# An mLSTM cell and a feed-forward block on one core: the first product by Strassen's algorithm in the second chunk too

## The chip, the cores and the metric

The kernel runs on one core of a Trainium2 chip. The metric is the device time of one execution in microseconds; lower is better. The engines are PE (TensorE, matrix products), DVE (VectorE), ACT (ScalarE), POOL (GpSimd) and SP (SyncE, which here only issues transfers). "PEld" in a profile is PE loading the stationary operand of a product.

## The reference

Two blocks follow each other. The first is an mLSTM cell over 4 batches, 8 heads, 768 time steps and head size 40; the second is a product, a sigmoid-approximated GELU and another product over the 3072 resulting rows of 320 numbers.

```python
for t in range(S):                                   # per batch and head
    m_new = maximum(f_gate[t] + m, i_gate[t])
    f_stab, i_stab = exp(f_gate[t] + m - m_new), exp(i_gate[t] - m_new)
    m = m_new
    C = f_stab * C + i_stab * outer(v[t], k[t])      # 40 x 40 state
    n = f_stab * n + i_stab * k[t]
    y[t] = sigmoid(o_gate[t]) * (C @ q[t]) / maximum(abs(n @ q[t]), 1)
x = y as (4*768, 8*40)
h = x @ w_in                                         # 320 x 2048
g = h / (1 + exp(-1.702 * h))
out = g @ w_out                                      # 2048 x 320
```

## The kernel before

**Chunks.** The 768 time steps are cut into NW = 6 chunks (`w`) of 128 steps; a chunk has 4 batches (`b`) of 128 rows, so 512 rows (tokens) of the feed-forward block. Within a chunk the recurrence is written as products: scores of queries and keys, weighted by a matrix of exponentials `wt` that masks the future, times the values, plus the state of the earlier chunks times the queries.

**The order of the work.** It is written out by hand: every engine executes its instructions in the order in which the program names them, and so does SP with its transfers. The main loop at the end of the kernel does, for each chunk `w`, the first product of the feed-forward block (`j` runs over 8 pairs of 128 hidden units), then the second product in blocks (`i`), and between these blocks the attention of chunk `w + 1`, in the steps that `attention(w + 1)` lists and at the block numbers in `stops`. In the first chunk the weights are still being loaded and converted: `fetch(n)` brings raw pieces into staging slots (`big`, six slots of 128 x 1024 numbers, and others), and `convert(n)` turns them into float32 weights with two operations on ACT and four on DVE. `beside` and `weights_in` say which piece is fetched and converted when.

**The first product.** Its contraction is over the 320 columns of a row: two full groups of 128 (`c`) and a rest of 64 (`w_in_x`). In the chunks 0 and 1 `up` computes it plainly: for each pair of hidden units two half columns (`i`) by two groups (`c`), each with all 512 tokens as moving operand. From the chunk 2 on `up_fast` takes Strassen's algorithm (in Winograd's form) for the two full groups: the operands are cut into 2 x 2 blocks (group or hidden half by group, group by token half), and seven products with 256 tokens take the place of eight. It needs sums of weights, `as1`, `as2`, `as4` and `a10` in place (`first_sums`, `first_difference`, made once, while the chunk 1 is worked on), and sums of the chunk's own transposed rows `xT`, `bt1`, `bt2`, `bt4` and `b01` in place (four DVE operations at its start). DVE and ACT add the products up.

**The second product.** In chunk 0 `down(w, b, n)` computes it plainly, in 16 blocks. From chunk 1 on `down_fast` takes Strassen's algorithm, in 7 blocks for each half `c` of the tokens: 14 blocks. It needs sums of weights, `t1`, `t2`, `t4` and `w01` in place (`weight_sums`), and sums of hidden units (`hidden_sums`, DVE). Each block's product goes to one of two banks of `ps_m`; DVE adds it to `o_sb` (line 629, or a copy in line 627), and SP stores the finished rows of one batch (line 633): `store(1)` at block 5 and `store(0)` at block 6 of each half. `o_sb` has two buffers, so the second half (from block 7 on) writes into buffers from which the first half is stored.

**Queries and keys.** `load_blocks(w)` brings the keys and queries of chunk `w` into `k_bl` and `q_bl` with 32 transfers, and `transposes(w, b)` turns one batch of each into `kT` and `qT` on DVE; `k_bl` and `q_bl` have one buffer each, so a chunk's load waits for the transposes of the chunk before it. `gates(w)` computes the running maxima and sends them to DRAM as `m_row`; `spread(w)` brings them back into `wt`, ACT takes the exponentials (line 335), and POOL masks them (line 337). `new_states(w)` (PE) and `carry(w)` (DVE, and a memset on POOL) bring the recurrent state forward: from chunk 2 on as a step of the attention, in chunk 1 in the middle of `up`. `seam(w, b)` transposes the attention's rows into `xT`.

Of the kernel before, what the change touches and what calls it, by code (L numbers as in the profile page):

```python
# [8 lines left out]
FP = mybir.dt.float32  # L9
U32 = mybir.dt.uint32  # L10
BF = mybir.dt.bfloat16
AF = mybir.ActivationFunctionType
OP = mybir.AluOpType
# [21 lines left out]
def kernel(  # L35
# [120 lines left out]
    def fetch(n):  # L156
        if 6 <= n < 10:
            bits[n] = gp.tile([128, 512, 2], U32, tag="g", name="bits")
        else:
            slot = n if n < 6 else (n - 10) % 6  # L160
            bits[n] = big[:, slot, :].bitcast(U32).rearrange("p (a two) -> p a two", two=2)
        for r, c, src in pieces[n][1]:
            dst = bits[n][r, c].rearrange("p a two -> p (a two)")
            if len(src.shape) == 3:
                dst = dst.rearrange("p (j m) -> p j m", j=src.shape[1])
            nc.sync.dma_start(out=dst, in_=src)
# [272 lines left out]
    def hidden_of(w, j):  # L439

        if j % 2 == 0:
            for i in range(2):
                gs[w, i * 4 + j // 2] = gp.tile([128, 2, W], FP, tag="g", name="g")
        return [gs[w, i * 4 + j // 2][:, j % 2, :] for i in range(2)]

    w_half = [[w_in_sb[:, c, :].rearrange("p (n h m) -> h p n m", h=2, m=256)[i] for c in range(2)] for i in range(2)]

    def up(w, j, n, states=False):


        x = xT[w].rearrange("p c b t -> p c (b t)")
        begin, end = range(j, j + n // 2), range(j + n // 2, j + n)
        ph = {}

        def take(j, pool, tag):
            ph[j] = [pool.tile([128, W], FP, tag=tag, name="p_h") for _ in range(2)]

        def full(j, first):
            for c in range(2):
                for i in range(2):  # L460
                    T.matmul(ph[j][i], w_half[i][c][:, j // 2, j % 2 * 128:(j % 2 + 1) * 128], x[:, c, :],  # L461
                             start=(first and c == 0), stop=(not first and c == 1))

        def rest(j, first):
            for i in range(2):
                r = slice(i * 64, i * 64 + 64)
                T.matmul(ph[j][i], w_in_x[r, j, :], x[r, 2, :], start=first, stop=not first)

        def gelu(j):
            for i, g in enumerate(hidden_of(w, j)):  # L470
                A.activation(out=g, in_=ph[j][i], func=AF.Gelu_apprx_sigmoid)  # L471

        for k in begin:
            take(k, *((ps_m, "m") if k == j else (ps_x, "x")))
            full(k, True)
        if states:
            new_states(w)
            carry(w)
        for k in begin:
            rest(k, False)  # L480
            gelu(k)
        for k in end:
            if k not in ph:
                take(k, *((ps_x, "x") if n == 2 else (ps_a, "a")))
            rest(k, True)
        for k in end:
            full(k, False)
            gelu(k)

    a00, a01, a10, a11 = w_half[0] + w_half[1]
    as1, as2, as4 = (big[:, i, :].rearrange("p (n m) -> p n m", m=256) for i in (3, 4, 5))

    def first_sums():
        V.tensor_tensor(out=as1, in0=a10, in1=a11, op=OP.add)
        V.tensor_tensor(out=as2, in0=as1, in1=a00, op=OP.subtract)
        V.tensor_tensor(out=as4, in0=a01, in1=as2, op=OP.subtract)

    def first_difference():  # L500
        V.tensor_tensor(out=a10, in0=a00, in1=a10, op=OP.subtract)

    def up_fast(w, j, between=None):
# [83 lines left out]
    w00, w01 = w_out_sb[:, 0:NH, 0:DH], w_out_sb[:, 0:NH, DH:DM]  # L587
    w10, w11 = w_out_sb[:, NH:NF, 0:DH], w_out_sb[:, NH:NF, DH:DM]

    def weight_sums():  # L590
        V.tensor_tensor(out=t1, in0=w01, in1=w00, op=OP.subtract)
        V.tensor_tensor(out=t2, in0=w11, in1=t1, op=OP.subtract)
        V.tensor_tensor(out=w01, in0=w11, in1=w01, op=OP.subtract)
        V.tensor_tensor(out=t4, in0=w10, in1=t2, op=OP.subtract)

    def hidden_sums(w, c, js, *what):

# [48 lines left out]
    def attention(w):  # L646
        if w > 1:

            return [[(columns, w)], [(weights, w, 0), (weights, w, 1)],
                    [(scores, w, 0), (hidden_sums, w - 1, 1, range(4), 3), (scores, w, 1), (weights, w, 2),  # L650
                     (weights, w, 3)],
                    [(values, w, 0), (values, w, 1), (scores, w, 2), (scores, w, 3)] +
                    [(scale, w, b) for b in (0, 1) if w + 1 < NW],
                    [(seam, w, 0), (seam, w, 1), (last_values, w)], [(carry, w)] if w + 1 < NW else [],
                    [(seam, w, 2)], [(seam, w, 3)]]
        steps = [[(columns, w)]]
        for s in range(B + 3):
            step = []
            for lag, f in ((3, seam), (2, values), (1, scores), (0, weights)):
                if 0 <= s - lag < B:  # L660
                    step.append((f, w, s - lag))
            if 0 <= s - 2 < B:
                step.append((scale, w, s - 2))
            steps.append(step)
        return steps

    def last_values(w):
# [95 lines left out]

    def next_keys():
        gates(w + 1)
        transposes(w + 1, 0)
        transposes(w + 1, 1)

    for w in range(NW):
        more = w + 1 < NW  # L770
        for j in range(NF // 2):
            if j % 2 == 0:
                if w:
                    if j % 4 == 0:
                        if w > 1:
                            up_fast(w, j, next_keys if more and j == 0 else None)
                        else:
                            up(w, j, 4, states=(j == 0))
                elif j == 0:
                    weights_in(0)  # L780
                    for pair_ in range(2):
                        for i, g in enumerate(hidden_of(0, pair_)):
                            A.activation(out=g, in_=first[pair_][i], func=AF.Gelu_apprx_sigmoid)
                else:
                    weights_in(j // 2)
                    up(w, j, 2, states=(j == 2))
            if j == 0 and more:
                load(w + 1, "o")
            if w == 0 and j == 0:
                load_blocks(1, 0)  # L790
                spread(1)
            if w == 1 and j == 1:
                weight_sums()
                first_sums()
            if more:
                if w == 1 and j == 0:
                    gates(w + 1)
                if j == 4:
                    if w == 0:
                        load_blocks(1, 1)  # L800
                    load(w + 1, "v")
                    if w:
                        spread(w + 1)
                if j == (4 if w else 6):
                    load(w + 1, "k")
                if w == 1 and 4 <= j < 6:
                    transposes(w + 1, 2 * j - 8)
                    transposes(w + 1, 2 * j - 7)
            if w > 1 and more and j == 3:
                transposes(w + 1, 2)  # L810
                transposes(w + 1, 3)
            if w and j in (3, 7):
                hidden_sums(w, 0, (j // 4 * 2, j // 4 * 2 + 1), 1, 2)
                if j == 3:
                    hidden_sums(w, 0, (0, 1), 3, 4)
        side = attention(w + 1) if more else []
        if w == 0:

            blocks = [(lambda b=b, n=n: down(w, b, n)) for ns in ((0, 1), (2,), (3,)) for b in range(B) for n in ns]
            stops = (0, 1, 5, 7, 9, 11, 13, 15)  # L820
        else:
            blocks = down_fast(w, 0) + down_fast(w, 1)
            stops = (0, 1, 2, 4, 8, 10, 11, 12)
        for i, block in enumerate(blocks):
            if w == 0:
                weights_in(4 + i)
                for b in {2: (0, 1), 7: (2,), 9: (3,)}.get(i, ()):
                    transposes(1, b)
            elif w + 2 < NW and i == 0:
                load_gates(w + 2)  # L830
                load_blocks(w + 2)
            block()
            if i in stops and side:
                run(side.pop(0))
            if w:
                for at, c, *what in ((0, 0, (2, 3), 3), (1, 0, (2, 3), 4), (1, 1, range(4), 1),
                                     (5, 1, range(2), 2), (6, 1, range(2, 4), 2), (7, 1, range(4), 4)):
                    if i == at:
                        hidden_sums(w, c, *what)
                if i == 2 and not more:  # L840
                    hidden_sums(w, 1, range(4), 3)
            if w == 1 and i == 9:
                first_difference()
        if w == 0:
            load_gates(2)
            load_blocks(2)


# [28 lines left out]
```

## Time and profile before

| | us |
|---|---|
| median of 13 runs | 492.01 |
| lowest and highest of them | 490.89, 495.15 |
| the profiled execution | 491.46 |
| its span in the profile | 489.8 |
| busy: PE, PEld | 482.5, 387.2 |
| busy: DVE, ACT, POOL | 328.8, 211.0, 60.7 |

Stretches of the profiled execution, as PE's timeline shows them, in microseconds from the start of the span:

| stretch | from | to | length |
|---|---|---|---|
| second product of chunk 0, with the attention of chunk 1 | 65.93 | 114.57 | 48.64 |
| first product of chunk 1 (plain) | 115.14 | 151.73 | 36.59 |
| second product of chunk 1, with the attention of chunk 2 | 151.73 | 195.92 | 44.19 |
| first product of chunk 2 (Strassen) | 195.92 | 228.02 | 32.10 |
| second product of chunk 2, with the attention of chunk 3 | 228.02 | 272.20 | 44.18 |

How to read profile lines: a timeline row gives start, length, engine, line of the kernel, operation, output <- inputs, shape and the number of instructions merged into the row; in brackets is how long the engine idled before it, and what ended that idle time. "SPq" is SP's queue of transfers; its length is the time of issue, not of the transfer. The slices of the page show the busy share of each engine in 40 equal parts of the span, in tenths.

### The profile page before, as it was taken

Reading aid. Unit: us, or ns where it says so; the run is one execution under the profiler, and the core shown is the slowest. Engines: PE = TensorE matmul, PEld = TensorE weight load, DVE = VectorE, ACT = ScalarE, POOL = GpSimd, SP = SyncE. Lnnn points to the kernel's source line nnn. Section 1 sums busy time; section 2 is a strip of 40 time slices with the busy share of each in tenths; the row PEclk is TensorE's granted clock in tenths of the full one; section 3 lists DMA queues with packets and bytes.
Section 4 is the critical chain, followed back from the end, with each engine's and each line's share of the span. In section 5 each row is a group of like instructions: output and inputs, shape, how many; then the busy total and the mean of one; then the engine's idle time right before and its main releaser. Section 6 shows DMA issues by size and latency. Waiting matters only on the chain. (4 is left out here: it accounts for less than half of the span.)

```text
span 489.8 us, 10267 instructions
## 1 busy us (share of the span) xinstructions
PE 482.5 (99%) x4028; PEld 387.2 (79%) x4028; DVE 328.8 (67%) x819; ACT 211.0 (43%) x535; POOL 60.7 (12%) x103
## 2 busy tenths in 40 slices
PE   8999999999999999999999999999999999999997
PEld 4874456774447999777999877999977999877897
DVE  8789765872983766677786596677666786254831
ACT  6766766301315600466800374900364930255300
POOL 4030001231000340000322000232000120000000
PEclk9999999999999999999999999999999999999999
DMA  9999799403699610896200696300294000000000
GB/s 132 182 277 352 90 271 168 55 28 63 74 240 132 75 32 15 127 239 67 27 28 3 103 257 80 33 29 2 63 264 37 2 1 28 28 0 3 0 28 27
DMA packets 175952, 44.85 MB, mean 92 GB/s; under 512 B 164352, under 2 KB 169504, under 8 KB 175904
## 3 DMA queue, kind: packets, MB, share of 16 engines
q1 hardware_dynamic: 175904, 44.21, 48.1%
q8 instruction: 31, 0.51, 0.4%
q14 instruction: 17, 0.14, 0.1%
HBM read 40.17 MB, written 4.01 MB: 90 GB/s over the span
## 5 line engine op out<-in xcount | busy, mean ns | idle before, releaser
L624 PE MATMUL p_out<-w_out_sb,g 128*128 128x160 f32 x480 | 69.8, 301 | 0.0
L624 PEld LDWEIGHTS p_out<-w_out_sb,g 128*128 128x128 f32 x480 | 66.4, 190 | 1.3 <-issue 0.5
L400 ACT COPY xT<-p_x 128x384 f32<-128x384 f32 x24 | 11.0, 481 | 128.4 <-PE p_x L399 128.4
L533 DVE TENSOR_TENSOR g<-p_u,g 128x256 f32<-128x256 f32 x64 | 27.2, 425 | 40.8 <-PE p_u L525 32.8
L337 POOL TENSOR_SCALAR_AFFINE_SELECT wt<-wt 128x1024 f32<-128x1024 f32 x20 | 22.5, 1123 | 226.8 <-ACT wt L335 195.8
L461 PE MATMUL p_h<-xT,w_in_sb 128*128 128x512 f32 x112 | 49.9, 599 | 0.6 <-ACT xT L400 0.6
L530 ACT COPY g<-p_u 128x256 f32<-128x256 f32 x96 | 34.5, 378 | 34.5 <-PE p_u L525 31.2
L629 DVE TENSOR_TENSOR o_sb<-o_sb,p_out 128x160 f32<-128x160 f32 x70 | 21.4, 317 | 41.2 <-PE p_out L624 40.9
L335 ACT ACTIVATE wt<-wt,cols 128x128 f32<-128x128 f32 x160 | 48.0, 395 | 0.0
L537 ACT ACTIVATE g<-g 128x256 f32<-128x256 f32 x96 | 33.9, 427 | 31.3 <-DVE g L533 31.3
L461 PEld LDWEIGHTS p_h<-xT,w_in_sb 128*128 128x128 f32 x112 | 20.7, 190 | 28.8 <-issue 26.8
L573 PE MATMUL p_out<-w_out_sb,g 128*128 128x320 f32 x128 | 36.2, 437 | 0.0
L350 DVE TENSOR_TENSOR wt<-p_s,wt 128x512 f32<-128x512 f32 x48 | 30.5, 683 | 8.4 <-POOL wt L337 6.3
L624 PE MATMUL p_out<-t,big 128*128 128x160 f32 x240 | 35.5, 301 | 0.0
L624 PEld LDWEIGHTS p_out<-t,big 128*128 128x128 f32 x240 | 33.3, 190 | 0.2
L471 ACT ACTIVATE g<-p_h 128x512 f32<-128x512 f32 x28 | 15.8, 598 | 38.1 <-PE p_h L461 20.0
L573 PEld LDWEIGHTS p_out<-w_out_sb,g 128*128 128x128 f32 x128 | 23.8, 190 | 10.1 <-issue 0.5
L525 PE MATMUL p_u<-xT,w_in_sb 128*128 128x256 f32 x128 | 31.2, 382 | 0.0
L525 PE MATMUL p_u<-xs,big 128*128 128x256 f32 x128 | 30.3, 379 | 0.0
L553 PE MATMUL p_u<-xT,w_in_x 64*128 64x512 f32 x64 | 29.6, 602 | 0.0
L553 PE MATMUL p_v<-xT,w_in_x 64*128 64x512 f32 x64 | 29.6, 602 | 0.0
L525 PEld LDWEIGHTS p_u<-xT,w_in_sb 128*128 128x128 f32 x128 | 23.7, 190 | 4.5 <-DVE o_sb L629 1.5
(166 smaller groups left out, 865.6 us busy)
## 6 DMA issues: line engine op xcount, KB each, us to landing
wt<-m_row SPq DMA_DIRECT2D x20, 512.0 KB, 6.7
out_dram<-o_sb SPq DMA_DIRECT2D x24, 160.0 KB, 1.8
eo<-in_o_gate_dram SPq DMA_DIRECT2D x5, 640.0 KB, 5.6
v_st<-in_v_dram SPq DMA_DIRECT2D x5, 640.0 KB, 8.8
k_st<-in_k_dram SPq DMA_DIRECT2D x5, 640.0 KB, 11.3
big<-in_moe_w_in_dram SPq DMA_DIRECT2D x5, 512.0 KB, 6.0
big<-in_moe_w_out_dram SPq DMA_DIRECT2D x8, 320.0 KB, 5.4
k_bl<-in_k_dram SPq DMA_DIRECT2D x40, 64.0 KB, 2.6
```

The lines of the kernel that those rows point to most:

```text
L335: A.activation(out=x[:, h, :], in_=x[:, h, :], func=AF.Exp, scale=-1.0, bias=cols[w][:, b * H + h:b * H + h + 1])
L337: G.affine_select(out=x, in_=x, compare_op=OP.is_ge, fill=0.0, base=0, pattern=[[0, H], [1, L]], channel_multiplier=-1)
L350: V.tensor_tensor(out=wt[w, b][:, :, i, :], in0=pw[i], in1=wt[w, b][:, :, i, :], op=OP.mult)
L461: T.matmul(ph[j][i], w_half[i][c][:, j // 2, j % 2 * 128:(j % 2 + 1) * 128], x[:, c, :], start=(first and c == 0), stop=(not first and c = ...
L525: T.matmul(p[k][:, ts[t]], a[:, k // 2, k % 2 * 128:(k % 2 + 1) * 128], b, start=first, stop=True, skip_group_check=True)
L530: A.copy(out=g[k][i][:, ts[t]], in_=chain[k][:, ts[0]])
L533: V.tensor_tensor(out=g[k][i][:, ts[t]], in0=p[k][:, ts[pt]], in1=g[k][i][:, ts[t]], op=OP.add)
L537: A.activation(out=dst, in_=dst if src is None else src, func=AF.Gelu_apprx_sigmoid)
L553: T.matmul(p[k], w_in_x[r, k, :], x[r, 2, :], start=False, stop=True, skip_group_check=True)
L573: T.matmul(po, gs[w, f // 2][:, f % 2, b * L:(b + 1) * L], w_out_sb[:, f, :], start=(f == 0), stop=(f == NF - 1))
L624: T.matmul(po, a(f), b[:, f, :], start=(f == 0), stop=(f == NH - 1))
L629: V.tensor_tensor(out=dst, in0=x, in1=po, op=OP.add)
```

## The change

The second chunk's first product goes by `up_fast` as well, so its weights' sums are made earlier:

- `first_sums`, with `first_difference` taken into it, runs in chunk 0's second product, ahead of block 2. It writes to other staging slots than before, and piece 19 of the weights, which used one of them, is staged in `xs`.
- `weight_sums` is cut into four calls: three at blocks 12, 14 and 15 of chunk 0's second product, one at `j == 3` of chunk 1's first product.
- `new_states(1)` and `carry(1)` become part of the last step of chunk 1's attention, which runs after the last block of chunk 0.
- Chunk 2's gates are computed at the start of `up_fast` in chunk 1. Its transposes are split: batches 0 and 1 at `j == 3` of chunk 1's first product, batches 2 and 3 ahead of blocks 2 and 3 of its second product.
- `load_gates(2)` goes from behind chunk 0's blocks to ahead of the first of them; `load_gates(3)` and `load_blocks(3)` go from block 0 of chunk 1 to block 4.
- `up` is left for chunk 0 alone and is shortened accordingly.

```diff
@@ -157,8 +157,8 @@
         if 6 <= n < 10:
             bits[n] = gp.tile([128, 512, 2], U32, tag="g", name="bits")
         else:
-            slot = n if n < 6 else (n - 10) % 6
-            bits[n] = big[:, slot, :].bitcast(U32).rearrange("p (a two) -> p a two", two=2)
+            room = xs if n == 19 else big[:, n if n < 6 else (n - 10) % 6, :]
+            bits[n] = room.bitcast(U32).rearrange("p (a two) -> p a two", two=2)
         for r, c, src in pieces[n][1]:
             dst = bits[n][r, c].rearrange("p a two -> p (a two)")
             if len(src.shape) == 3:
@@ -445,15 +445,12 @@
 
     w_half = [[w_in_sb[:, c, :].rearrange("p (n h m) -> h p n m", h=2, m=256)[i] for c in range(2)] for i in range(2)]
 
-    def up(w, j, n, states=False):
-
-
-        x = xT[w].rearrange("p c b t -> p c (b t)")
-        begin, end = range(j, j + n // 2), range(j + n // 2, j + n)
-        ph = {}
-
-        def take(j, pool, tag):
-            ph[j] = [pool.tile([128, W], FP, tag=tag, name="p_h") for _ in range(2)]
+    def up(j, states):
+
+
+        x = xT[0].rearrange("p c b t -> p c (b t)")
+        ph = {k: [pool.tile([128, W], FP, tag=tag, name="p_h") for _ in range(2)]
+              for k, pool, tag in ((j, ps_m, "m"), (j + 1, ps_x, "x"))}
 
         def full(j, first):
             for c in range(2):
@@ -467,37 +464,28 @@
                 T.matmul(ph[j][i], w_in_x[r, j, :], x[r, 2, :], start=first, stop=not first)
 
         def gelu(j):
-            for i, g in enumerate(hidden_of(w, j)):
+            for i, g in enumerate(hidden_of(0, j)):
                 A.activation(out=g, in_=ph[j][i], func=AF.Gelu_apprx_sigmoid)
 
-        for k in begin:
-            take(k, *((ps_m, "m") if k == j else (ps_x, "x")))
-            full(k, True)
+        full(j, True)
         if states:
-            new_states(w)
-            carry(w)
-        for k in begin:
-            rest(k, False)
-            gelu(k)
-        for k in end:
-            if k not in ph:
-                take(k, *((ps_x, "x") if n == 2 else (ps_a, "a")))
-            rest(k, True)
-        for k in end:
-            full(k, False)
-            gelu(k)
+            new_states(0)
+            carry(0)
+        rest(j, False)
+        gelu(j)
+        rest(j + 1, True)
+        full(j + 1, False)
+        gelu(j + 1)
 
 
 
     a00, a01, a10, a11 = w_half[0] + w_half[1]
-    as1, as2, as4 = (big[:, i, :].rearrange("p (n m) -> p n m", m=256) for i in (3, 4, 5))
+    as1, as2, as4 = (big[:, i, :].rearrange("p (n m) -> p n m", m=256) for i in (4, 5, 3))
 
     def first_sums():
         V.tensor_tensor(out=as1, in0=a10, in1=a11, op=OP.add)
         V.tensor_tensor(out=as2, in0=as1, in1=a00, op=OP.subtract)
         V.tensor_tensor(out=as4, in0=a01, in1=as2, op=OP.subtract)
-
-    def first_difference():
         V.tensor_tensor(out=a10, in0=a00, in1=a10, op=OP.subtract)
 
     def up_fast(w, j, between=None):
@@ -587,11 +575,9 @@
     w00, w01 = w_out_sb[:, 0:NH, 0:DH], w_out_sb[:, 0:NH, DH:DM]
     w10, w11 = w_out_sb[:, NH:NF, 0:DH], w_out_sb[:, NH:NF, DH:DM]
 
-    def weight_sums():
-        V.tensor_tensor(out=t1, in0=w01, in1=w00, op=OP.subtract)
-        V.tensor_tensor(out=t2, in0=w11, in1=t1, op=OP.subtract)
-        V.tensor_tensor(out=w01, in0=w11, in1=w01, op=OP.subtract)
-        V.tensor_tensor(out=t4, in0=w10, in1=t2, op=OP.subtract)
+    def weight_sums(n):
+        out_, in0, in1 = ((t1, w01, w00), (t2, w11, t1), (t4, w10, t2), (w01, w11, w01))[n]
+        V.tensor_tensor(out=out_, in0=in0, in1=in1, op=OP.subtract)
 
     def hidden_sums(w, c, js, *what):
 
@@ -662,6 +648,7 @@
             if 0 <= s - 2 < B:
                 step.append((scale, w, s - 2))
             steps.append(step)
+        steps[-1] += [(new_states, w), (carry, w)]
         return steps
 
     def last_values(w):
@@ -763,38 +750,31 @@
 
     def next_keys():
         gates(w + 1)
-        transposes(w + 1, 0)
-        transposes(w + 1, 1)
+        if w > 1:
+            transposes(w + 1, 0)
+            transposes(w + 1, 1)
 
     for w in range(NW):
         more = w + 1 < NW
         for j in range(NF // 2):
-            if j % 2 == 0:
-                if w:
-                    if j % 4 == 0:
-                        if w > 1:
-                            up_fast(w, j, next_keys if more and j == 0 else None)
-                        else:
-                            up(w, j, 4, states=(j == 0))
-                elif j == 0:
-                    weights_in(0)
-                    for pair_ in range(2):
-                        for i, g in enumerate(hidden_of(0, pair_)):
-                            A.activation(out=g, in_=first[pair_][i], func=AF.Gelu_apprx_sigmoid)
-                else:
-                    weights_in(j // 2)
-                    up(w, j, 2, states=(j == 2))
+            if w == 0 and j == 0:
+                weights_in(0)
+                for pair_ in range(2):
+                    for i, g in enumerate(hidden_of(0, pair_)):
+                        A.activation(out=g, in_=first[pair_][i], func=AF.Gelu_apprx_sigmoid)
+            elif w == 0 and j % 2 == 0:
+                weights_in(j // 2)
+                up(j, j == 2)
+            elif w and j % 4 == 0:
+                up_fast(w, j, next_keys if more and j == 0 else None)
             if j == 0 and more:
                 load(w + 1, "o")
             if w == 0 and j == 0:
                 load_blocks(1, 0)
                 spread(1)
-            if w == 1 and j == 1:
-                weight_sums()
-                first_sums()
+            if w == 1 and j == 3:
+                weight_sums(3)
             if more:
-                if w == 1 and j == 0:
-                    gates(w + 1)
                 if j == 4:
                     if w == 0:
                         load_blocks(1, 1)
@@ -803,12 +783,9 @@
                         spread(w + 1)
                 if j == (4 if w else 6):
                     load(w + 1, "k")
-                if w == 1 and 4 <= j < 6:
-                    transposes(w + 1, 2 * j - 8)
-                    transposes(w + 1, 2 * j - 7)
-            if w > 1 and more and j == 3:
-                transposes(w + 1, 2)
-                transposes(w + 1, 3)
+                if w and j == 3:
+                    for b in range(2) if w == 1 else range(2, 4):
+                        transposes(w + 1, b)
             if w and j in (3, 7):
                 hidden_sums(w, 0, (j // 4 * 2, j // 4 * 2 + 1), 1, 2)
                 if j == 3:
@@ -824,9 +801,15 @@
         for i, block in enumerate(blocks):
             if w == 0:
                 weights_in(4 + i)
+                if i == 0:
+                    load_gates(2)
+                if i == 2:
+                    first_sums()
                 for b in {2: (0, 1), 7: (2,), 9: (3,)}.get(i, ()):
                     transposes(1, b)
-            elif w + 2 < NW and i == 0:
+            elif w == 1 and i in (2, 3):
+                transposes(2, i)
+            if w and w + 2 < NW and i == (4 if w == 1 else 0):
                 load_gates(w + 2)
                 load_blocks(w + 2)
             block()
@@ -839,10 +822,9 @@
                         hidden_sums(w, c, *what)
                 if i == 2 and not more:
                     hidden_sums(w, 1, range(4), 3)
-            if w == 1 and i == 9:
-                first_difference()
+            elif i in (12, 14, 15):
+                weight_sums((12, 14, 15).index(i))
         if w == 0:
-            load_gates(2)
             load_blocks(2)
 
 
```

## The prediction

> **What bounds the kernel now.** I read the page's head and slices first, then PE's timeline around the second chunk, then the timelines of the queues that feed it. Starts and lengths are microseconds of the profiled execution.
>
> ```profile
> span 489.8 us, 10267 instructions
> ...
> PE 482.5 (99%) x4028; PEld 387.2 (79%) x4028; DVE 328.8 (67%) x819; ACT 211.0 (43%) x535; POOL 60.7 (12%) x103
> ...
> PE   8999999999999999999999999999999999999997
> ```
>
> PE is in use from end to end, so every microsecond of matmul removed counts, and so does every new PE gap. DVE has spare time only in places. PE's timeline:
>
> ```profile
> 115.14 7.13 PE L461 MATMUL p_h<-xT,w_in_sb 128*128 128x512 f32 x16 [0.57 <-ACT xT L400]
> 122.20 1.43 PE L425 MATMUL p_c<-v_st,k_st 128*40 128x41 f32 x64
> ...
> 151.73 2.34 PE L624 MATMUL p_out<-w_out_sb,g 128*128 128x160 f32 x16
> ...
> 195.92 2.14 PE L525 MATMUL p_u<-xT,w_in_sb 128*128 128x256 f32 x8
> ```
>
> The second chunk (w=1) has its plain first product from 115.14 to 151.73; its second product follows; the third chunk's Strassen product runs from 195.92 to 228.02, where its second product begins. DVE's timeline, from four places, and two rows of POOL's:
>
> ```profile
> 73.28 0.70 DVE L302 STREAM_TRANSPOSE kT<-k_bl 128x512 f32<-128x512 f32 x1
> 78.92 0.71 DVE L302 STREAM_TRANSPOSE qT<-q_bl 128x512 f32<-128x512 f32 x1 [4.94 <-DMA q_bl<-in_q_dram]
> ...
> 161.15 2.31 DVE L605 TENSOR_TENSOR g<-g 128x256 f32<-128x256 f32 x4
> ...
> 237.48 1.42 DVE L605 TENSOR_TENSOR g<-g 128x256 f32<-128x256 f32 x4
> ...
> 331.21 0.56 DVE L627 COPY o_sb<-p_out 128x160 f32<-128x160 f32 x2 [1.96 <-DMA out_dram<-o_sb]
> ```
>
> ```profile
> 73.85 1.09 POOL L337 TENSOR_SCALAR_AFFINE_SELECT wt<-wt 128x1024 f32<-128x1024 f32 x1 [30.98 <-DMA q_bl<-in_q_dram]
> ...
> 162.08 1.10 POOL L337 TENSOR_SCALAR_AFFINE_SELECT wt<-wt 128x1024 f32<-128x1024 f32 x1 [2.18 <-ACT wt L335]
> ```
>
> In the first chunk's second product DVE has a 4.94 hole, waiting for queries, and PE runs into that wait: its scores start at 79.69, 0.34 idle ahead of them. The two L605 rows show another thing: the same four SBUF-to-SBUF sums took 2.31 where POOL's select began among them (162.08) and 1.42 in the next chunk, where it began only at their end. The last DVE row, in the fourth chunk, is a copy into o_sb that waited for an earlier store to land. SP's queue in w=1:
>
> ```profile
> 151.52 9.85 SPq L117 DMA_DIRECT2D k_bl<-in_k_dram  x16
> 161.47 9.66 SPq L117 DMA_DIRECT2D q_bl<-in_q_dram  x16
> 174.67 22.13 SPq L633 DMA_DIRECT2D out_dram<-o_sb  x4
> ```
>
> One load_blocks holds SP for 17 to 20 us, 0.53 for most transfers. Stores leave by the same queue, behind it.
>
> **The product itself.** Plain: 36.59 from 115.14 to 151.73, of which 1.36 (122.20 to 123.56) is new_states, that stays; and 0.57 of idle ahead of it. Strassen: 32.10, the same in the third and fourth chunk. In the new order new_states follows the last transposes at 114.50, and its 1.36 covers the copy of xT that PE waited for; the first Strassen products read only earlier columns. So 36.59 + 0.57 - 1.36 - 32.10 = **3.70 off the path**. ACT's busy time in the stage rises from 9.56 to some 17.1, DVE's adds come in at 0.42 each; the third chunk shows PE unbroken over the same load, so they cost nothing.
>
> **Before the product: DVE.** After the last copy of p_out (114.28) DVE now has carry (2.05), one weight sum (1.49) and the sums of xT. carry can begin 0.93 after new_states (as 123.13 against 122.20), at 115.4; 115.4 + 2.05 + 1.4 + 0.9 puts bt2 at 119.8. PE wants it 3.70 into the product (195.92 to 199.62), at 115.86 + 3.70 = 119.56. Cost 0.3 (0 to 0.6). The two weight sums at i=12 and 14 fit holes of 1.43 and 1.50 where DVE waited for PE: nothing; if POOL's v_st and state scaling (0.73 each) pushes the second, copy 15 is 0.7 later, before PE wants its bank.
>
> **The first weights' sums at i=2.** Three of 1.22 and one of 1.23, back to back 4.9: 73.28 to 78.2, the hole almost exactly, with kT to follow by 78.85 and qT at 78.92 as before. That is the cover. But all four read two SBUF operands, and two selects of POOL (73.85 and 77.34, 1.09 each) fall among them. The pair 2.31 against 1.42 says that such a select takes 0.9 from DVE; by its own length, 1.1. Two of them: sums end at 80.0 to 80.4, then kT and qT (1.3), PE's scores start at 81.3 to 81.7 and not at 79.69. I take **1.8**; bounds 0 (no delay) and 2.0. Nothing later gives it back: PE has no idle in that stage.
>
> **Moved DVE and SP work in w=1.** weight_sums(3) (1.49) and two transposes (2.7) after the first half compare with 2.7 in the third chunk, where DVE then idled 3.59: covered. Their qT needs q_bl: load_blocks(2) still begins behind the last store, its 17.7 of issue and some 2.5 of landing end 20.5 after that store; DVE can wait until then with under 1 to spare. Cost 0, up to 0.5 if the cover fails. load_gates(2) goes ahead of the stores of w=0 on SP, which idled there; gates(2) puts m_row ahead of the o load: nothing waits for either by name. Slot 3 of big goes to as4, fetch(19) goes to xs, free since the first chunk's attention: nothing. first_difference leaves i=9: DVE saves 1.23 off the path.
>
> **load_gates(3) and load_blocks(3) from i=0 to i=4 of w=1: the costly move.** Thirty-four transfers. They may overwrite k_bl only after transposes(2,3), at i=3. Clock from the start of this second product (151.73 before, or 228.02 in the third chunk, whose pace applies since its Strassen product precedes it). transposes(2,2) at i=2 uses idle time ahead of the L350 pair; L350 for b=1 waits for POOL as before and ends near 13.2; kT(2,3) ends near 14.0. From there the 32 loads: 17.2 to 19.5, I take 17.6: 31.6. Before, they were through at 19.4 (171.13). Store(1) of the first half was ready at 174.65, or 22.9: it now stands on SP behind the loads until 31.6, and lands 1.8 to 3.9 later (I take 2.2): **33.8**. The copies of block 7 (25.45 before) wait for that landing, and DVE is in order: behind them stand the s4 sums (1.4), block 8's add (0.3), both value chains (5.45) and block 9's add. Block 11 on PE needs block 9's bank: landing + 0.5 + 1.4 + 0.3 + 5.45 + 0.3 = 33.8 + 7.9 = 41.7, against 37.01 before (188.74). So **+4.6**, after 0.1 off because POOL no longer collides with the chain. PE first idles about 2 at block 9, then about 3 at block 11. Bounds: 13.7 + 17.2 + 1.8 gives 3.3; 14.3 + 19.5 + 3.9 gives 8.6. The value chosen is near the lower bound since three of four clean issues took 17.2 to 17.7.
>
> The gaps have one more side. In the trace the granted clock is 1.00 in every stage and, after the start, no PE gap exceeds 0.6, so no row prices a gap of 2 to 3; my sum has none for it. The Trainium skill (TensorE: Matmul & The Clock Gate, "Why this matters for your kernels") warns of idle gaps above some 3 us, after which TensorE falls back to half clock. By it the sum would stay as it is for these gaps, and would rise by an estimated 1.7 (half of a 3.4 us window) if one reached the limit.
>
> **Sum.** -3.70 + 0.3 + 1.8 + 4.6 = **+3.0**. The profiled execution took 491.46 (span 489.8, 1.66 around it), so 494.5; the median of 13 is 0.55 above it, 492.01, so I predict **495.0**. A measurement here can tell about 0.2%, 0.98 us, from no change.
>
> **Rivals.** (A) Faster: the stores get out in time. The place is SP's queue at store(1); the point is a landing at 29.1, that is, the loads issued in about 13 (0.40 each) or an o buffer that is free anyway. Then -3.70 + 0.3 + 1.8 = -1.6: 490.4. For it: in w=1 the copy at 177.18 waited for PE alone. Against: at 331.21 it did wait for the store, and 0.53 per transfer holds in all four load_blocks read. (B) POOL doesn't hold the sums: -3.70 + 0.3 + 4.6 = +1.2: 493.2; against it stands the 2.31 row. (C) Neither cost: -3.4: 488.6. (D) Loads with the hitches of w=1 (19.5) and a store of 3.9: +7: 499.
>
> **Chances.** Forecast 0.64 (its costs at their ends give 493 to 498), A 0.11, B 0.17, C 0.03, D 0.05. Faster is A and C, 0.14. B's lower part (landing bound 3.3 gives 492.0) makes 0.10 for no change; the rest, 0.76, is slower. The range 491.9 to 498.0 holds forecast and B; A, C and D, 0.19, are left out.
>
> **What would show it.** Right: Strassen product of w=1 in 32.1 with new_states right before it; an idle of about 2 on PE before the scores of w=1, b=0, put down to DVE qT; SP's 32 loads starting some 14 into the second product of w=1, the first two stores behind them, DVE's L627 with a wait of 8 or so for DMA, and two PE gaps behind it. Wrong: the copies of block 7 at about 25 into that product, or the first sums through by 78.3.

## The result, and the profile after

The changed kernel takes 496.76 us (median of 11 runs, 494.53 to 501.12), the kernel before 491.60 (48 runs): a ratio of 1.0096, 95% interval 1.0078 to 1.0115. It is slower by about 5 us. The profiled execution took 496.62, with a span of 494.9. The head of its page and two rows of its slices:

```profile
span 494.9 us, 10439 instructions
...
PE 481.7 (97%) x4076; PEld 398.0 (80%) x4076; DVE 343.2 (69%) x855; ACT 220.9 (45%) x575; POOL 62.7 (13%) x103
...
PE   8999998999999978999999999999999999999997
PEclk9999999999999998999999999999999999999999
```

PE's busy time fell by only 0.8 (482.5 to 481.7), although the shorter product takes out 3.13 of it (36.59 - 1.36 - 32.10; the rest of the 3.70 was idle time). Three slices of PE newly stand below 9, with an 8, a 7 and an 8. In the last of them the granted clock drops as well, which it does in no slice of the page of before. PE's timeline of the changed kernel (start, length, operation, idle time before it and what ended it):

```profile
81.01 1.16 PE L348 MATMUL p_s<-qT,kT 40*128 40x128 f32 x16 [1.73 <-DVE qT L302]
...
115.82 1.43 PE L425 MATMUL p_c<-v_st,k_st 128*40 128x41 f32 x64
117.18 1.99 PE L513 MATMUL p_u<-xT,w_in_sb 128*128 128x256 f32 x8
...
121.22 1.97 PE L513 MATMUL p_u<-xs,big 128*128 128x256 f32 x8 [0.31 <-issue]
...
149.69 2.34 PE L610 MATMUL p_out<-w_out_sb,g 128*128 128x160 f32 x16
...
185.23 2.44 PE L610 MATMUL p_out<-t,big 128*128 128x160 f32 x16 [2.92 <-DVE o_sb L613]
...
192.12 3.28 PE L610 MATMUL p_out<-t,xs 128*128 128x160 f32 x16 [2.27 <-DVE o_sb L615]
...
201.07 2.14 PE L513 MATMUL p_u<-xT,w_in_sb 128*128 128x256 f32 x8
```

New_states stands right ahead of the Strassen product, which takes 32.51 (117.18 to 149.69) with its one small wait at 121.22. The three waits above 1 us are new. L613 and L615 are the lines 627 and 629 of the kernel before. From the third chunk's first product on (here 201.07, before 195.92) the two executions take the same time, so the whole difference lies ahead of it:

| stretch on PE, us | before | after | difference |
|---|---|---|---|
| start to chunk 0's second product | 65.93 | 65.86 | -0.07 |
| to the scores of chunk 1 | 13.76 | 15.15 | +1.39 |
| to the first product of chunk 1 | 35.45 | 36.17 | +0.72 |
| first product of chunk 1 | 36.59 | 32.51 | -4.08 |
| second product of chunk 1 | 44.19 | 51.38 | +7.19 |
| sum | 195.92 | 201.07 | +5.15 |

In the third and fourth row new_states (1.36) has changed sides, so they are read together: -3.36.

The first sums on DVE, and POOL's selects among them:

```profile
73.20 1.22 DVE L486 TENSOR_TENSOR big<-w_in_sb 128x1024 f32<-128x1024 f32 x1
74.45 1.99 DVE L487 TENSOR_TENSOR big<-big,w_in_sb 128x1024 f32<-128x1024 f32 x1
76.48 1.23 DVE L488 TENSOR_TENSOR big<-w_in_sb,big 128x1024 f32<-128x1024 f32 x1
77.63 2.11 DVE L489 TENSOR_TENSOR w_in_sb<-w_in_sb 128x1024 f32<-128x1024 f32 x1
...
184.62 0.56 DVE L613 COPY o_sb<-p_out 128x160 f32<-128x160 f32 x2 [10.05 <-DMA out_dram<-o_sb]
```

The same copy in the kernel before, 25.45 us into the product:

```profile
177.18 0.56 DVE L627 COPY o_sb<-p_out 128x160 f32<-128x160 f32 x2 [0.56 <-PE p_out L624]
```

POOL's selects in the changed kernel:

```profile
73.79 1.59 POOL L337 TENSOR_SCALAR_AFFINE_SELECT wt<-wt 128x1024 f32<-128x1024 f32 x1 [30.98 <-DMA q_bl<-in_q_dram]
77.28 1.38 POOL L337 TENSOR_SCALAR_AFFINE_SELECT wt<-wt 128x1024 f32<-128x1024 f32 x1 [1.91 <-ACT wt L335]
```

Two of the four equal sums take 1.99 and 2.11 and not 1.22, and the selects take 1.59 and 1.38 where they took 1.09. Each select begins during one sum, which keeps its 1.22 or 1.23, and ends during the next, which is the long one. The copy waited 10.05 for the first half's store, where it had waited 0.56 for PE. SP's queue in the same stage shows why: the loads are through at 182.18, and the stores stand behind them.

```profile
163.60 9.22 SPq L117 DMA_DIRECT2D k_bl<-in_k_dram  x16
172.93 9.25 SPq L117 DMA_DIRECT2D q_bl<-in_q_dram  x16
182.60 19.35 SPq L619 DMA_DIRECT2D out_dram<-o_sb  x4
```

Last, the busy times and the granted clock (the column PEclk, 1.00 is full) in three stretches around PE's second gap:

```profile
core 0: us, PE busy (x) PEld busy (x) DVE busy (x) ACT busy (x) POOL busy (x), PEclk, DMA share, GB/s
188.00:192.00 4.00, 1.85 (x14) 1.60 (x12) 3.62 (x12) 0.00 (x0) 0.34 (x2) 1.00 0.00 0
...
193.60:196.90 3.30, 3.30 (x16) 3.26 (x14) 1.35 (x4) 0.48 (x1) 0.00 (x0) 0.50 0.01 2
197.00:200.00 3.00, 3.00 (x25) 3.00 (x24) 0.32 (x1) 0.48 (x1) 0.00 (x0) 1.00 0.01 3
```

After the gap the clock is halved from 193.56 for 3.41 us. A block of 16 products that takes 2.17 from start to next start elsewhere takes 2.74 to 3.07 here. In 10 of the 12 recorded executions of the changed kernel the mean clock over the span is below 0.999.

### The profile page after: what moved, and what is told of

Its sections match the earlier page's. It is cut to its first block, busy times and chain, and to the rows that moved or that the text cites. A ratio compares the mean times of both kernels' runs of the same rounds, so it can differ in the third digit from the quotient of the medians.

```text
span 494.9 us, 10439 instructions
## 1 busy us (share of the span) xinstructions
PE 481.7 (97%) x4076; PEld 398.0 (80%) x4076; DVE 343.2 (69%) x855; ACT 220.9 (45%) x575; POOL 62.7 (13%) x103
## 5 line engine op out<-in xcount | busy, mean ns | idle before, releaser
L521 DVE TENSOR_TENSOR g<-p_u,g 128x256 f32<-128x256 f32 x80 | 34.0, 425 | 47.0 <-PE p_u L513 37.0
L518 ACT COPY g<-p_u 128x256 f32<-128x256 f32 x120 | 43.1, 378 | 42.8 <-PE p_u L513 38.6
L525 ACT ACTIVATE g<-g 128x256 f32<-128x256 f32 x120 | 42.4, 427 | 39.1 <-DVE g L521 39.1
L615 DVE TENSOR_TENSOR o_sb<-o_sb,p_out 128x160 f32<-128x160 f32 x70 | 21.3, 317 | 43.3 <-PE p_out L610 42.9
L513 PE MATMUL p_u<-xT,w_in_sb 128*128 128x256 f32 x160 | 38.9, 382 | 0.0
L513 PE MATMUL p_u<-xs,big 128*128 128x256 f32 x160 | 38.0, 380 | 0.3 <-issue 0.3
L541 PE MATMUL p_u<-xT,w_in_x 64*128 64x512 f32 x80 | 37.0, 602 | 0.0
L541 PE MATMUL p_v<-xT,w_in_x 64*128 64x512 f32 x80 | 37.0, 602 | 0.0
L513 PEld LDWEIGHTS p_u<-xs,big 128*128 128x128 f32 x160 | 29.9, 190 | 5.3 <-issue 0.7
L521 DVE TENSOR_TENSOR g<-p_v,g 128x256 f32<-128x256 f32 x80 | 29.8, 415 | 0.0
L541 PEld LDWEIGHTS p_v<-xT,w_in_x 64*128 64x128 f32 x80 | 14.2, 186 | 17.4 <-issue 17.4
```

Of the source, the lines that this page charges most:

```text
L513: T.matmul(p[k][:, ts[t]], a[:, k // 2, k % 2 * 128:(k % 2 + 1) * 128], b, start=first, stop=True, skip_group_check=True)
L518: A.copy(out=g[k][i][:, ts[t]], in_=chain[k][:, ts[0]])
L521: V.tensor_tensor(out=g[k][i][:, ts[t]], in0=p[k][:, ts[pt]], in1=g[k][i][:, ts[t]], op=OP.add)
L525: A.activation(out=dst, in_=dst if src is None else src, func=AF.Gelu_apprx_sigmoid)
L541: T.matmul(p[k], w_in_x[r, k, :], x[r, 2, :], start=False, stop=True, skip_group_check=True)
L615: V.tensor_tensor(out=dst, in0=x, in1=po, op=OP.add)
```

## The experiments

The theory: three costs of some 1.4 to 5.4 us each outweigh the 3.4 that the product gains: the loads in front of the stores, the selects beside the first sums, and half clock with the gaps that these leave. The main rival: Strassen's extra sums on DVE and the moved transposes, not the loads, delay the second half of the second product. Edits are made to the changed kernel unless said otherwise. The times of the kernel before beside these runs had medians of 492.05 (first four experiments) and 491.95 (last four).

**The loads behind the stores.** The same loads, begun at block 7, when the first half's stores have been named.

```diff
-            if w and w + 2 < NW and i == (4 if w == 1 else 0):
+            if w and w + 2 < NW and i == (7 if w == 1 else 0):
```

> The changed kernel with load_gates(3) and load_blocks(3) issued ahead of block 7 of the second chunk's second product, behind the two stores of blocks 5 and 6, and not ahead of block 4. Theory (the two stores stood behind 32 loads on SP, the copies of block 7 waited for one of them, PE for the copies and then for the value chain): that product shrinks from 51.4 us to 44.2 to 44.6, PE's gaps of 2.9 and 2.3 go, the granted clock of the whole execution is 1.00, the time falls by some 7, to 489.5. Rival 1 (the moved transposes load DVE too much): the transposes stay, so the product stays near 51 and the time near 496.8. Rival 2 (the loads collide with whatever runs beside them): part of the loss comes back in the next first product, which grows from 32.1 to 34 or more.

Measured: 491.26 (10 runs, 489.25 to 494.22), ratio 0.9977 (0.9944 to 1.0009). The second product takes 44.18 (154.51 to 198.69, the last two rows of the first fence below), as in the kernel before (44.19). So all of the 7.19 came from this position of the loads, half clock included, and nothing of it from the sums or the moved transposes, which stayed. The expected time of 489.5 and full clock were missed, because of another stage. PE's timeline, and the stretch behind the scores of chunk 1 (columns as above):

```profile
82.67 1.66 PE L348 MATMUL p_s<-qT,kT 40*128 40x128 f32 x12 [3.25 <-DVE qT L302]
...
154.51 2.34 PE L610 MATMUL p_out<-w_out_sb,g 128*128 128x160 f32 x16
...
198.69 1.49 PE L513 MATMUL p_u<-xT,w_in_sb 128*128 128x256 f32 x5
```

```profile
82.50:89.20 6.70, 6.53 (x25) 4.74 (x26) 5.44 (x11) 1.24 (x2) 0.00 (x0) 0.50 1.12 236
```

In this execution the loads of the program's start ran late and the wait ahead of the scores was 3.25 and not 1.73; half clock followed for 6.8 us. Of the 10 executions, the 3 at a mean clock of 0.999 or more took 489.25 to 489.69, the other 7 490.88 to 494.22. (For the kernel before beside it, 18 of 24 had the full clock.)

**The stores past the loads.** The loads stay where the change put them, but the first half's stores leave by ACT's queue.

```diff
-            nc.sync.dma_start(out=out[b * S + w * L:b * S + (w + 1) * L, :], in_=o[two])
+            (A if w == 1 and c == 0 else nc.sync).dma_start(out=out[...], in_=o[two])
```

> The changed kernel with the two stores of the first half of the second chunk's second product issued from ACT's queue; the loads stay ahead of block 4. Theory (only the order in SP's queue holds the stores): the stores leave at about 23 and 24 us into that product, the copies of block 7 do not wait, the product takes 44.2 to 44.8, the time is some 7 below the changed kernel, 489.5. Rival (the transfers themselves are slow while 32 loads are under way, whatever the queue): the copies of block 7 still wait several us for the landing, and the product stays above 47.

Measured: 490.69 (10 runs, 489.41 to 494.26), ratio 0.9969 (0.9932 to 1.0006), and the second product takes 44.18 again (149.82 to 194.00). ACT's queue and DVE:

```profile
172.75 1.64 ACTq L619 DMA_DIRECT2D out_dram<-o_sb  x2
```

```profile
175.27 0.56 DVE L613 COPY o_sb<-p_out 128x160 f32<-128x160 f32 x2 [0.57 <-PE p_out L610]
```

The loads begin at 163.73, as in the changed kernel (163.60), the stores go at 172.75 in the middle of them, and the copy that waited 10.05 for its store now waits 0.57 for PE. So it is the order on one queue that costs, not the transfers as such, nor their share of the DMA engines. A third buffer for `o_sb`, the other way to free the copy, wasn't tried.

**No select beside the sums.** POOL's select is left out for the batches 0 and 1 of chunk 1, whose weights are then not masked.

```diff
+        if w > 1 or b > 1:
             G.affine_select(out=x, in_=x, compare_op=OP.is_ge, fill=0.0, base=0, ...)
```

> The changed kernel without the causal mask (POOL's select) for batches 0 and 1 of the second chunk. Theory (POOL's select and sums with two SBUF operands take turns): the four first sums take 4.9 us in place of 6.5, PE's wait ahead of the scores falls from 1.73 to 0.4 or less, the time by 1.3. Rival (the sums are slower there for another reason, such as the transfers into the staging slots): the sums stay at 6.3 or more and the wait at 1.6 or more.

Measured: 494.65 (8 runs, 493.35 to 499.45), ratio 1.0060 (1.0023 to 1.0097). On DVE:

```profile
74.81 1.23 DVE L488 TENSOR_TENSOR big<-big,w_in_sb 128x1024 f32<-128x1024 f32 x1
...
77.22 1.22 DVE L490 TENSOR_TENSOR w_in_sb<-w_in_sb 128x1024 f32<-128x1024 f32 x1
```

These are the two sums that took 1.99 and 2.11 (the lines stand one lower here); they take 1.23 and 1.22, and all four 4.9. That part is shown. The wait ahead of the scores came to 1.08 and not to 0.4 or less: in this execution the sums began 0.61 later, counted from the start of the second product of chunk 0 (65.61, in the changed kernel 65.86), and the transpose behind them waited another 0.29 for queries. So the removal of the selects gave back the sums' 1.66, but not all of it reached the path. The median fell by 2.1, more than the 1.3 expected; in the two profiled executions 1.03 of the 1.93 lies behind the scores, where PE had one gap of 3.08 with half clock in place of the two gaps, and is no effect of the sums.

**A filler in the second gap.** Ten products on data without use ahead of block 11, to keep PE busy while it waits.

```diff
+            if w == 1 and i == 11:
+                keep_busy(10)
             block()
```

> The changed kernel with ten idle matmuls (bf16, 512 columns, some 2.1 us, no result used) on PE ahead of block 11 of the second chunk's second product, so that they run in PE's second gap of 2.3 us. Theory (the clock falls because PE stood idle): granted clock 1.00 in all or nearly all runs where the changed kernel shows 0.993 to 0.996 in most; block 11 takes 2.2 us and not 3.1; the time is 1 to 2 below the changed kernel, 495. Rival (the first gap of 2.9 alone sets it off, or the drop has nothing to do with the gaps): clock and block 11 as in the changed kernel, time 496.5 to 498.

Measured: 498.05 (4 runs, 496.22 to 498.56), ratio 1.0111 (1.0071 to 1.0151): no faster. PE's timeline and the stretch behind it:

```profile
193.08 2.32 PE L188 MATMUL p_idle<-idle 128*128 128x512 bf16 x10
195.51 2.44 PE L610 MATMUL p_out<-t,xs 128*128 128x160 f32 x16
```

```profile
194.00:200.00 6.00, 5.89 (x40) 4.93 (x39) 4.09 (x12) 0.48 (x1) 0.33 (x2) 1.00 0.00 1
```

In the stage it did what was expected: the clock stays full, and the second product takes 48.83, 2.55 less than 51.38 (0.88 of it because the first gap was 2.04 here and not 2.92). But the wait ahead of the scores was 3.26 in this execution and drew half clock there, and all four executions have a mean clock of 0.997. The expected full clock and lower time did not come, and as a time the run settles nothing; the following filler stands where it turned out to be needed.

**A filler ahead of the scores.** The loads at block 7, as above, and eight such products ahead of the scores of chunk 1.

```diff
+        if w == 1 and b == 0:
+            keep_busy(8)
```

> The kernel with the loads behind block 6's store, and eight idle matmuls (bf16, 512 columns, some 1.7 us, no result used) on PE ahead of the scores of chunk 1, batch 0, where PE waits 1.7 to 3.3 us. Theory (half clock comes from PE standing idle there): the granted clock is 0.999 to 1.00 in nearly all runs, where without the filler seven of ten showed 0.993 to 0.997; median 489.5 to 490.5 against 491.3. Rival (the drop has another cause): the clocks are as mixed as without the filler, median 491 or more.

Measured: 490.04 (12 runs, 489.19 to 492.96), ratio 0.9952 (0.9921 to 0.9982). PE idles 0.21 and not 1.73 to 3.25 ahead of the scores:

```profile
81.53 1.16 PE L350 MATMUL p_s<-qT,kT 40*128 40x128 f32 x16 [0.21 <-DVE qT L302]
```

The scores come no earlier, 15.36 after the start of the second product (15.15 in the changed kernel). Yet 11 of 12 executions have a mean clock of 0.999 or more, against 3 of 10 without the filler; the kernel before had 18 of 22 beside the former and 18 of 24 beside the latter, so the two chips on which these versions ran hardly differ in this. The pair shows that idle time of PE takes the clock down.

**The move alone.** The kernel before, with the plain product and all sums where they were, given only the moved transposes of batches 2 and 3 (blocks 2 and 3) and the loads at block 4.

> The kernel before with one part of the change alone: transposes(2,2) and (2,3) moved to blocks 2 and 3 of the second chunk's second product, load_gates(3) and load_blocks(3) to block 4; the first product stays plain. Theory (this move by itself makes the wait): that product grows from 44.2 us to 49.5 to 52 with the same two PE gaps of 2 to 3 us, the half clock appears after them in part of the runs, the time is 5 to 7 above the kernel before, 497 to 499. Rival (the move costs only together with the Strassen product ahead of it): the product stays at 44 to 45, the time within 1 of the kernel before.

Measured: 499.46 (4 runs, 497.91 to 501.19), ratio 1.0148 (1.0111 to 1.0184), the slowest of all; its second product takes 50.98. On PE:

```profile
188.73 4.64 PE L624 MATMUL p_out<-t,big 128*128 128x160 f32 x16 [4.19 <-DVE o_sb L627]
```

One gap of 4.19 in place of two, and block 9 behind it takes 4.64 where 2.44 is usual, since the clock is halved; it fell while PE was still waiting. So the move costs some 6.8 us without any of Strassen's work in it, and the main rival falls from the other side as well.

**Eight loads later.** Twenty-four of the 32 loads at block 4, the last eight (half of the queries) at block 7.

> The changed kernel with 24 of the 32 loads left ahead of block 4 and the last eight behind block 6's store. Theory (the stage has a slack: a landing at 29.1 us into the product costs nothing, every us past it costs one): 24 loads end at 13.9 + 12.9 = 26.8, the store lands at 28.6 to 29.5, so the product takes 44.2 to 44.8. Rival (any loads ahead of the stores cost in proportion): three quarters of 5.4 us stay, the product takes 48 or more.

Measured: 492.71 (8 runs, 490.48 to 496.25), ratio 1.0009 (0.9979 to 1.0039). The copies come at 181.35, 29.5 into the second product, as the count of loads says. The product takes 45.97, 1.2 over what was expected. DVE:

```profile
181.83 3.07 DVE L591 TENSOR_TENSOR big<-g,big 128x256 f32<-128x256 f32 x4
```

These four sums, 1.42 elsewhere, took 3.07: at their new time POOL was scaling `v_st` and the state, from 181.20 to 184.62. That POOL caused it fits the selects above, but was not tried by itself. So neither expectation held: a delay is not merely handed on; it may bring DVE beside other work of POOL. Ahead of the scores PE waited 2.32 in this execution, and the clock was halved for 3.41 us there.

**Three remedies at once.** Loads at block 7; the fourth of the first sums (`a10`) only at block 7 of chunk 0, behind the transposes; and the third weight sum (`t4`) from block 15 into the start of chunk 1's `up_fast`.

```diff
+                if i == 7:
+                    first_difference()
...
-            if w and w + 2 < NW and i == (4 if w == 1 else 0):
+            if w and w + 2 < NW and i == (7 if w == 1 else 0):
...
+        if w == 1:
+            weight_sums(2)
...
-            elif i in (12, 14, 15):
+            elif i in (12, 14):
```

> The changed kernel with three moves: the loads behind block 6's store; the fourth of the first weights' sums (a10) behind the transposes at block 7 of the first chunk; the sum t4 from block 15 into the start of the Strassen product, behind the gates. Theory: PE's wait ahead of the scores falls from 1.73 to 0.4 (three sums end with the arrival of the queries), the wait of 0.3 in the product goes, the second product takes 44.2; span of an undisturbed execution 486.1, time 487.8; the granted clock is 1.00 in most runs, and the median is 488 to 489.5, 0.6% to 0.8% below the kernel before. Rival (the sums moved to later places make DVE late there): a new wait of over 0.5 at block 8 or 9 of the first chunk or in the product, and the time no better than that of the kernel with the loads alone moved, 491.

Measured: 487.24 (6 runs, 486.97 to 487.78), ratio 0.9900 (0.9876 to 0.9924): faster than both kernels, 1.0% below the kernel before. PE's timeline:

```profile
79.86 1.16 PE L348 MATMUL p_s<-qT,kT 40*128 40x128 f32 x16 [0.56 <-DVE qT L302]
...
116.03 1.99 PE L515 MATMUL p_u<-xT,w_in_sb 128*128 128x256 f32 x8
...
147.98 2.34 PE L612 MATMUL p_out<-w_out_sb,g 128*128 128x160 f32 x16
...
192.16 2.14 PE L515 MATMUL p_u<-xT,w_in_sb 128*128 128x256 f32 x8
```

The wait ahead of the scores is 0.56, the Strassen product takes 31.95, the second product 44.18, and all six executions have the full clock; the expected wait of 0.4 was not quite reached, and the time came 0.8 below the expected range. What each of the three moves gave was not measured apart, except for the loads. Its span of 486.0 is 3.8 below that of the kernel before, next to the 3.70 of the product that the prediction worked out.

## Why the prediction was right, and where it was off

The direction and its main cause were right, and the time is 1.76 above the predicted 495.0. The difference fits less well than the time: 5.16 between the medians against a forecast of 3.0, and the time is as near as it is partly by luck, because the median of the kernel before, 491.60 in its 48 runs, was 0.41 below the 492.01 that the prediction stood on. The two executions of the changed kernel at full clock took 494.53 and 495.88. By its terms, in the profiled executions:

- **The product, -3.70, and the wait for bt2, +0.3.** Measured -3.36 together, against -3.40. The third chunk's row was a fair price; the small wait stands at 121.22 with 0.31; the row puts it down to issue, but DVE's second sum of `xT`, expected at 119.8, ended at 121.11, just before it.
- **First sums, +1.8.** Measured +1.39. The two sums lost 0.77 and 0.89, 1.66 together, against the 0.9 each that the prediction took from the pair 2.31 and 1.42 of the trace before. What was not foreseen is that POOL pays as well (0.50 and 0.29): by the starts and ends of the rows, the two take turns. The Trainium skill (GPSIMD Engine Reference, "8. Key points") says that GpSimd shares its interfaces to SBUF, the on-chip memory, with VectorE and contends with instructions of two SBUF inputs. The section gives no price; the rows here do.
- **The loads at block 4, +4.6 (3.3 to 8.6).** Measured +7.19. The loads began 13.91 into the product (taken: 14.0), took 18.6 (17.6), and the copies followed at 34.93 (33.8), 1.1 late. From there to block 11 it was 7.50 (7.9), 0.4 early. So block 11 began at 42.43, 5.42 later than in the kernel before (37.01). The rest, 1.77, is half clock on blocks 11 and 12 and the transposes between them, which the sum had at zero. (Added up again from the prediction's own numbers, its bounds are 3.5 and 8.5, not 3.3 and 8.6.)
- **So the term that was most mis-sized is the clock**, nothing against 1.77; the loads without it were 0.8 short. The sum stood on "no row prices a gap of 2 to 3" and set it at nothing. PE's gaps were foreseen as some 2 and 3 and came as 2.92 and 2.27, 5.2 in all against 5; in this execution it was the shorter one that was followed by half clock. The 1.7 that stood beside the sum is what one such stretch does cost here, half of 3.41.
- **The edits costed at nothing** (the gates, the weight sums at blocks 12 and 14, `weight_sums(3)`, the transposes) cost nothing that shows: from the scores of chunk 1 to its second product the sum of the rows is -3.36 against -3.40, and the second product takes 44.18 with all of them in place once the loads are moved. The weight sum at block 15 runs on DVE right before the sums of `xT` (118.83, 1.49) and may carry the small wait in the Strassen product, which takes 31.95 without that wait in the version where it was moved away; that was not tried alone.

Of the rivals, A's condition (the stores get out in time) did not come true in the changed kernel, but was made true by two edits, which took 491.26 and 490.69 against its 490.4; at full clock they took 489.62 and 489.64 in the median. B's condition (POOL takes nothing) is refuted by the rows with and without the selects. C, both at once, was put at 488.6; the three remedies, which remove most of both costs, took 487.24.

What stays open is the exact rule of the clock. The kept traces hold six half-clock stretches after the program's start, each of 3.41 or 6.83 us and each with a PE gap. Read in steps of 0.1 us (all in us; "idle before" is PE's idle time in the 3.41 before the clock fell):

| run | gap | clock fell | idle before | half clock for |
|---|---|---|---|---|
| changed kernel, second gap | 2.27 | 1.44 after the gap's end | 1.98 | 3.41 |
| eight loads later | 2.32 | 0.69 after it | 2.32 | 3.41 |
| filler in the second gap, at the scores | 3.26 | 1.42 after it | 1.99 | 3.41 |
| loads at block 7, at the scores | 3.25 | 0.26 before it | 2.99 | 6.83 |
| no select | 3.08 | 0.66 before it | 2.42 | 6.83 |
| the move alone | 4.19 | 1.79 before it | 2.40 | 6.83 |

If one lays a grid of 3.41 us along the edges of the changed kernel's stretch, its 2.92 gap, after which the clock stayed full, falls into two cells, with at most 1.91 in one. So the rows agree with a measure of idle time per fixed stretch, with a limit of some 1.9 to 2.0 us in one cell, and with half clock lasting one stretch longer where the next one still begins with idle time. This is argued from these cases and was not tested by itself.

## What to carry to other kernels

A long batch of transfers holds back every later transfer of its queue (here 32 loads took 18.6 us to issue, and two stores behind them waited for that), so ask of every moved load which stores are named behind it, and count from the store's landing to the next writer of its buffer. A saving on PE is only kept if PE stays busy: a wait of 2 to 3 us on the critical engine costs its own length and, here, in most executions another 1.7 to 3.4. When you price work that is put into a hole of a helper engine, look for what another engine does in the same memory at that time, and price both.

## What the runs showed of the hardware

- Half clock set in with gaps of 2.27 to 4.19 us, for 3.41 us (2.27, 2.32 and 3.26) or 6.83 us (3.08, 3.25 and 4.19). The Trainium skill (TensorE: Matmul & The Clock Gate, "Why this matters for your kernels") sets the limit at gaps of about 3 us. Here a gap of 2.27 was enough and one of 2.92 was not, so the length of a gap alone does not decide.
- The same page ("What's actually happening") says that the window of some 3.4 us runs freely. That agrees with the 3.41 and 6.83 of these traces, and with the changing clock of executions of one kernel (0.993 to 1.00).
- Products on unused data in a gap keep the clock: 11 of 12 executions at full clock with eight of them ahead of the scores, 3 of 10 without.
- DVE sums with two SBUF operands and POOL's selects beside them lengthen each other: 1.22 became 1.99 and 2.11, POOL's 1.09 became 1.59 and 1.38; without the selects the sums took 1.22 and 1.23. Four sums beside POOL's scalings took 3.07 in place of 1.42, which was not tried without the scalings.
- Transfers named behind others on SP's queue wait for their issue: 32 loads held it for 18.58 us, and the copy that needed the store behind them waited 10.05. With the same stores on ACT's queue it waited 0.57, for PE.
